# A cached attention and MLP decode step on one core: weight-stage matmuls taken round four column tiles, GELU in thirds, down-projection as four partial sums

## The chip, the cores and the metric

The kernel runs on one core of a Trainium2 chip. The metric is device time in microseconds (us); lower is better. Times quoted are medians of several executions, all of them undisturbed ("fast"). The profile is one further execution, traced; its span is 1 to 2 us shorter than the timed value, because the span runs from the first to the last instruction. Engine names in profile lines: PE is TensorE, PEld its weight loads, DVE is VectorE, ACT is ScalarE, POOL is GpSimd, SP is the engine that issues the large loads.

## The reference, cut to what matters

```python
# x: [8,1,576]   k_cache, v_cache: [8, 32, 4096, 128]   all bf16
g = sigmoid((x * gate_w).sum(-1, keepdims=True))
q = (x @ wq) -> [8, 32 heads, 1, 128]
p = softmax(q @ k_cache^T * 128**-0.5)
a = (p @ v_cache) -> [8,1,4096] @ wo            # attention branch
y = layernorm(x)
h = gelu(y @ w1 + b1)                            # [8,1,4608]
b = h @ w2 + b2                                  # MLP branch
out = g * a + (1 - g) * b
```

The two caches hold 2 x 268 MB = 537 MB. The four weight matrices hold 20 MB. Every byte is used once, so nearly all of the work is reading.

## The kernel before

SBUF holds three slots. The first three loads put wq, w1 and w2 into them; later each slot takes one block of K or V (8.39 MB: eight heads of one batch entry). There are 32 such groups, so 64 block loads, all issued by SP in order, each as soon as the slot that it overwrites is free:

```python
def load_kv(kind, g):
    n = n_load[0]; n_load[0] += 1
    s = n % 3                                        # three slots in turn
    ...
    land[kind, g] = op("sync", lambda e: e.dma_start(slot[s][:, :, :], src), free[n - 3], dma=dma)
```

The order is K0, K1, V0, K2, V1, K3, V2 and so on. K0 takes wq's slot (free when Q is done), K1 takes w1's (free when the up-projection is done), V0 takes w2's (free when the down-projection is done).

The part that the change rewrites is the weight stage, which comes before the first scores. All its matmuls have only 8 useful output rows (the batch), so four results are kept side by side on PSUM partitions 0, 32, 64 and 96. Those are the four *column tiles* of the array:

```python
    for half in range(2):                            # Q projection
        for h in range(4):                           # column tile
            for kt in range(NKT):                    # 5 matmuls in a row on one tile
                o = tr_ps[half][32 * h:32 * h + B, :]
                ... matmul(o, lhsT=xT_sb[:, xi, :], rhs=wq part, start=(kt == 0), stop=(kt == NKT - 1))
    ...
    for k in range(3):                               # up-projection
        for c in range(4):                           # column tile
            o = up_ps[32 * c:32 * c + B, k, 0:FB]
            for kt in range(NKT):                    # 5 matmuls, 128 rows high
                ... matmul(o, lhsT=yT_sb[:, yi, :], rhs=w1 part, start=(kt == 0), stop=False)
            p_up = matmul(o, lhsT=one1[:, :], rhs=b1_row[:, col:col + FB], start=False, stop=True)  # bias: 1 row high
    ...
    # GELU of all of h at once: 4 VectorE passes of 104x1152, a sigmoid on ScalarE, 1 VectorE pass
    # 36 small matmuls transpose h; 4 VectorE copies
    for jt in range(NJ):                             # down-projection, already round the four tiles
        p_down = quarters(hT_sb[:, jt, :], w2_sb[:, jt, :], jt == 0, False, ...)
```

In the loop, one group multiplies K by q on VectorE (8 pieces), sums over the head dimension with matmuls against the identity, reduces on VectorE, finds the maximum, takes exp on ScalarE and multiplies by V on TensorE. The softmax had six small VectorE operations in a chain, one of which only changed a sign.

Of the kernel before, what the change touches and what calls it, by code (L numbers as in the profile page):

```python
# [5 lines left out]
ACT = mybir.ActivationFunctionType  # L6
# [5 lines left out]
B = 8  # L12
# [178 lines left out]
def bass_gated_mix__mha_block_cached__mixer_channel_mlp__decode_kernel(  # L191
# [76 lines left out]
    b2_8 = late.take([B, D])  # L268
    b2_f = late.take32([B, D])
# [6 lines left out]
    zs = sb("zs", [32, 1], F32)  # L276
    acc = sb("acc", [128, GL, HB], F32)
# [11 lines left out]
    diag2 = sb("diag2", [B, 2, B], F32)  # L289
    g4 = sb("g4", [128, 2], F32)  # L290
    g32 = sb("g32", [32, 2, B], F32)
    ident = sb("ident", [128, 128], BF16)
    hneg = sb("hneg", [128, HB], F32)
# [5 lines left out]
    mC = sb("mC", [128, 32], F32)  # L299
# [5 lines left out]
    rz = sb("rz", [128, 1], F32)  # L305
# [11 lines left out]
    g32_ps = bank[3][0:32, 64:64 + 2 * B]  # L317
    ht_ps = PS[:, 0:NJ * 32].rearrange("p (j c b) -> p j c b", j=NJ, c=4)
    xt_ps = bank[7]
# [30 lines left out]
    ld_b2 = load("scalar", b2_8, bcast(B_b2, 0, D), "ld_b2")  # L350
# [55 lines left out]
    c_hneg = op("vector", lambda e: e.tensor_scalar(out=hneg[:, :], in0=hsel[:, ::NDQ], scalar1=-1.0, scalar2=60000.0,  # L406
# [10 lines left out]
    c_selq = op("vector", lambda e: e.tensor_copy(  # L417
# [4 lines left out]
    c_b2 = op("gpsimd", lambda e: e.tensor_copy(out=b2_f, in_=b2_8), [ld_b2])  # L422
    c_sp8 = op("vector", lambda e: e.tensor_copy(
# [4 lines left out]
    c_Sel = op("vector", lambda e: e.tensor_copy(  # L428
# [36 lines left out]
    def untransposed(dst, col, waits):  # L465
        return op("vector", lambda e: e.tensor_copy(
            out=dst.rearrange("p k b -> p (k b)"), in_=xt_ps[:, col:col + (NKF + 2) * B]), waits)
# [9 lines left out]
    v_dg = op("vector", lambda e: e.tensor_tensor(  # L477
        out=diag2[:], in0=bass.AP(tensor=ident, offset=0, ap=[[pstride(ident), B], [0, 2], [1, B]]),
        in1=bass.AP(tensor=stat, offset=G_COL, ap=[[pstride(stat), B], [1, 2], [0, B]]), op=ALU.mult), [v_omg, c_id])
# [5 lines left out]
    t = op("tensor", lambda e: e.matmul(g32_ps, lhsT=ones8[:, :], rhs=diag2[:].rearrange("k s b -> k (s b)"),  # L485
                                        start=True, stop=True), [c_one8])
    v_g4 = op("vector", lambda e: e.tensor_copy(out=g4[:, :], in_=g4_ps), [t])
    v_g32 = op("vector", lambda e: e.tensor_copy(out=g32[:].rearrange("p s b -> p (s b)"), in_=g32_ps), [t])
# [3 lines left out]
    for half in range(2):  # L492
        for h in range(4):
            for kt in range(NKT):
# [12 lines left out]

    for k in range(3):
        for c in range(4):
            col = c * FC + k * FB  # L510
            o = up_ps[32 * c:32 * c + B, k, 0:FB]
            for kt in range(NKT):
                r = w1_sb[:, kt, col:col + FB] if kt < NKF else w1_t[:, col - (c // 2) * (F // 2):][:, 0:FB]
                yi = kt if kt < NKF else NKF + c // 2
                p_up = op("tensor", lambda e, o=o, r=r, kt=kt, yi=yi: e.matmul(  # L515
                    o, lhsT=yT_sb[:, yi, :], rhs=r, start=(kt == 0), stop=False),
                    [v_yT, *ld_w1, *c_ps] if c == kt == k == 0 else ())
            p_up = op("tensor", lambda e, o=o, col=col: e.matmul(  # L518
                o, lhsT=one1[:, :], rhs=b1_row[:, col:col + FB], start=False, stop=True), [ld_b1, c_one1])
    free[1] = [p_up]  # L520
    h = up_ps[0:QP, :, 0:FB]
    t3 = t2[0:QP, :].rearrange("p (k n) -> p k n", k=3)
    t = op("vector", lambda e: e.tensor_copy(out=t3, in_=h), [p_up])  # L523
    t = op("vector", lambda e: e.tensor_tensor(out=t3, in0=t3, in1=h, op=ALU.mult), [t])
    t = op("vector", lambda e: e.tensor_scalar(out=t3, in0=t3, scalar1=0.044715, scalar2=1.0, op0=ALU.mult, op1=ALU.add), [t])
    t = op("vector", lambda e: e.tensor_tensor(out=t3, in0=t3, in1=h, op=ALU.mult), [t])
    t = op("scalar", lambda e: e.activation(out=t3, in_=t3, func=ACT.Sigmoid, scale=gelu_c), [t])
    v_h = op("vector", lambda e: e.scalar_tensor_tensor(
        out=hrow[0:QP, :].rearrange("p (k n) -> p k n", k=3), in0=h, scalar=g4[0:QP, 1:2], in1=t3,
        op0=ALU.mult, op1=ALU.mult), [t, v_g4])  # L530
    v_hb, v_hrow = [v_h], [v_h]
# [9 lines left out]
    def quarters(lhsT, w, first, stop, waits):  # L541

        for i in range(4):
            last = op("tensor", lambda e, i=i: e.matmul(  # L544
                y_ps[32 * i:32 * i + B, 0:QN], lhsT=lhsT, rhs=w[:, i * QN:(i + 1) * QN], start=first, stop=stop),
                waits if i == 0 else ())
        return last

    for jt in range(NJ):
        p_down = quarters(hT_sb[:, jt, :], w2_sb[:, jt, :], jt == 0, False,  # L550
                          [ld_w2, *v_hT, v_yT] if jt == 0 else ())
    for i in range(4):
        p_b2 = op("tensor", lambda e, i=i: e.matmul(
            y_ps[32 * i:32 * i + B, 0:QN], lhsT=diag2[:, 1, :], rhs=b2_f[:, i * QN:(i + 1) * QN], start=False, stop=False),
            [c_b2, v_dg])
    free[2] = [p_b2]
# [242 lines left out]
```

## Time and profile before

| | before |
|---|---|
| time, median of 6 runs | 1295.47 us |
| profiled span | 1293.2 us |
| read from memory | 556.96 MB |
| TensorE, VectorE busy | 57%, 63% |
| DMA share and rate, 5 to 1285 us | 1.00, 433 GB/s |
| first scores start | 59.9 us |

The page of the kernel before. Its first line gives busy time, share of the span and instruction counts; the second is the DMA's busy share in 40 slices, in tenths; the last shows which engines make up the chain of waits that ended last.

```profile
PE 733.4 (57%) x4926; PEld 337.1 (26%) x4926; DVE 819.7 (63%) x873; ACT 161.0 (12%) x587; POOL 40.4 (3%) x60
DMA  9999999999999999999999999999999999999998
HBM read 556.96 MB, written 0.01 MB: 431 GB/s over the span
DMA 54%; DVE 26%; PE 14%; ACT 5%; issue 1%; SPq 0%; ACTq 0%; DVEq 0%
```

No compute engine is busy for more than two thirds of the time, and the DMA row has no hole before its last slice. The last line invites a mistake. It gives VectorE 26% and TensorE 14% of the chain, as if 40% of the span could be had by speeding them up.

The table by windows of the kernel before: stretch, its length, busy time (and instructions) of PE, PEld, DVE, ACT and POOL, TensorE's granted clock, DMA share, GB/s.

```profile
5.00:1285.00 1280.00, 729.89 (x4791) 334.43 (x4792) 816.87 (x867) 159.16 (x584) 38.48 (x46) 0.85 1.00 433
1288.00:1290.00 2.00, 1.57 (x92) 1.19 (x80) 0.00 (x0) 0.00 (x0) 0.00 (x0) 1.00 0.49 191
1290.00:1294.00 4.00, 0.31 (x12) 0.11 (x8) 0.59 (x2) 0.54 (x2) 0.00 (x0) 0.98 0.02 4
```

From 5 to 1285 us the 16 DMA engines have no free time at all. After about 1290 us they have nothing left to do. So the span is roughly 2 us before the bytes flow, 1287 us of full DMA, and 3 us of last arithmetic and the store of the result.

The timeline of the kernel before, weight stage: start, duration, engine, source line, operation, output and inputs, shapes, count, and in brackets the engine's idle time before it and what ended that.

```profile
14.99 5.59 PE L499 MATMUL PS<-SL 128*8 128x512 bf16 x40 [1.01 <-DMA SL<-in_A_wq_dram]
...
32.45 0.98 PE L515 MATMUL PS<-SL 128*8 128x384 bf16 x5
33.36 0.32 PE L518 MATMUL PS<-SL,one 1*8 1x384 bf16 x1
33.61 0.98 PE L515 MATMUL PS<-SL 128*8 128x384 bf16 x5
...
54.97 3.96 PE L544 MATMUL PS<-SL 128*8 128x144 bf16 x144 [2.07 <-DVE SL L538]
...
59.50 0.28 ACT L572 ACTIVATE q_bc<-PS 128x128 bf16<-128x128 f32 x1 [10.41 <-PE PS L569]
...
59.89 4.49 DVE L580 TENSOR_TENSOR SL<-SL,q_bc 128x4096 bf16<-128x4096 bf16 x2 [5.06 <-DMA SL<-in_A_k_cache_dram]
```

L499 is the Q projection, L515 the up-projection, L518 its bias, L544 the down-projection, L572 the copy that makes the first q ready, and L580 the first multiplication of K by q.

The timeline of SP in the kernel before: the issues of K and V blocks. The first line merges two issues; the second of them starts at 20.62 + 22.68 - 0.33 = 42.97 us.

```profile
20.62 22.68 SPq L384 DMA_DIRECT2D SL<-in_A_k_cache_dram  x2
59.34 0.33 SPq L384 DMA_DIRECT2D SL<-in_A_v_cache_dram  x1
84.42 0.33 SPq L384 DMA_DIRECT2D SL<-in_A_k_cache_dram  x1
111.47 0.33 SPq L384 DMA_DIRECT2D SL<-in_A_v_cache_dram  x1
```

One block takes 8.39 MB / 433 GB/s = 19.4 us to move. In the loop a K block takes 43.4 us (median) from issue to landing, so a load spends over half of that waiting behind the loads before it. That is the mistake hidden in the chain of waits: the chain steps from a load back to whatever freed its slot, although the load would not have landed any sooner if the slot had come free earlier.

### The profile page before, as it was taken

To read this page: it belongs to the slowest core of one execution; us is meant where nothing else is said; L and a number is where in the kernel's file an instruction comes from. 1 tells how busy PE (TensorE), PEld (TensorE's weight loads), DVE (VectorE), ACT (ScalarE), POOL (GpSimd) and SP (SyncE) were. 2 spreads that over 40 slices of the span, in tenths; PEclk is the share of its full clock that TensorE was granted. 3 is DMA by queue.
4 is the path that set the end of the run, shared out by engine and by line. 5 is a ranking of instruction groups with operands and counts; after the bars stand their busy time and mean duration, and the time that the engine had idled before them with its cause. 6 is when DMAs were issued, how large, how long until landed. Compare 5 with 4: busy or idle time off the path is not lost.

```text
span 1293.2 us, 11790 instructions
## 1 busy us (share of the span) xinstructions
PE 733.4 (57%) x4926; PEld 337.1 (26%) x4926; DVE 819.7 (63%) x873; ACT 161.0 (12%) x587; POOL 40.4 (3%) x60
## 2 busy tenths in 40 slices
PE   3666566555556555556555556555556555556646
PEld 1322223122223222223222223222223222223223
DVE  2387567665567665567665567765567765567762
ACT  1011110111110011110011110011111011111011
POOL 1001000000000000000000000000000000000000
PEclk8799898878898887898787899778888877888888
DMA  9999999999999999999999999999999999999998
GB/s 406 427 447 424 439 430 436 432 430 436 434 428 436 436 432 438 430 438 432 430 436 434 428 436 438 430 438 430 438 430 432 436 432 434 432 438 430 436 424 366
DMA packets 10591, 557.16 MB, mean 431 GB/s; under 512 B 1201, under 2 KB 1233, under 8 KB 1745
## 3 DMA queue, kind: packets, MB, share of 16 engines
q1 hardware_dynamic: 10528, 556.94, 99.6%
q8 instruction: 9, 0.15, 0.0%
q10 hardware_dynamic: 50, 0.04, 0.0%
q14 instruction: 4, 0.03, 0.0%
HBM read 556.96 MB, written 0.01 MB: 431 GB/s over the span
## 4 chain that ended last, share of the span: by engine, by line
DMA 54%; DVE 26%; PE 14%; ACT 5%; issue 1%; SPq 0%; ACTq 0%; DVEq 0%
DMA SL<-in_A_k_cache_dram 50%; DVE SL L580 20%; PE PS L585 7%; DVE s_sb L591 5%; ACT P L625 4%; PE PS L640 4%; DMA SL<-in_B_w_dram 2%; DMA SL<-in_A_wo_dram 2%; PE PS L515 1%; PE PS L656 1%; ACT O_sb L645 1%; PE PS L544 0%; PE PS L518 0%; PE PS L649 0%; PE PS L535 0%
## 5 line engine op out<-in xcount | busy, mean ns | idle before, releaser
L585 PE MATMUL PS<-SL,ident 128*128 128x512 bf16 x2048 | 547.7, 420 | 518.3 <-DVE SL L580 518.3
L580 DVE TENSOR_TENSOR SL<-SL,q_bc 128x4096 bf16<-128x4096 bf16 x256 | 582.0, 2284 | 313.6 <-DMA SL<-in_A_k_cache_dram 313.6
L585 PEld LDWEIGHTS PS<-SL,ident 128*128 128x128 bf16 x2048 | 199.0, 106 | 853.8 <-DVE SL L580 614.8
L591 DVE TENSOR_REDUCE s_sb<-PS 128x32 f32<-128x512 f32 x256 | 175.8, 687 | 90.4 <-PE PS L585 90.3
L625 ACT ACTIVATE P<-s_sb,hb 128x256 bf16<-128x256 f32 x256 | 126.2, 494 | 663.3 <-PE PS L640 645.5
L640 PE MATMUL PS<-SL,P 128*32 128x512 bf16 x2048 | 128.5, 389 | 0.0
L640 PEld LDWEIGHTS PS<-SL,P 128*32 128x32 bf16 x2048 | 96.4, 138 | 17.9 <-issue 3.1
L564 POOL TENSOR_SCALAR Qm<-Q,sel 128x256 bf16<-128x256 bf16 x33 | 33.7, 1020 | 896.6 <-ACT O_sb L645 845.2
L572 ACT ACTIVATE q_bc<-PS 128x128 bf16<-128x128 f32 x33 | 9.1, 277 | 407.4 <-PE PS L569 407.4
L625 ACT ACTIVATION_READ_ACCUMULATOR P<-s_sb,hb 128x1 f32 x256 | 47.7, 186 | 0.0
L656 PE MATMUL PS<-O_sb,selq 128*32 128x128 f32 x256 | 34.2, 278 | 0.7 <-ACT O_sb L645 0.7
L656 PEld LDWEIGHTS PS<-O_sb,selq 128*32 128x32 f32 x256 | 26.0, 113 | 1.4 <-ACT O_sb L645 1.2
L645 ACT ACTIVATE O_sb<-PS 128x512 f32<-128x512 f32 x32 | 18.4, 574 | 10.0 <-PE PS L640 10.0
L523 DVE COPY SL<-PS 104x1152 f32<-104x1152 f32 x1 | 1.4, 1357 | 28.7 <-PE PS L518 28.7
L515 PE MATMUL PS<-SL 128*8 128x384 bf16 x60 | 13.2, 356 | 6.8 <-DMA SL<-in_B_w_dram 6.8
L669 DVE SCALAR_TENSOR_TENSOR On<-PS,rz,dqm 32x128 f32<-32x128 f32 x32 | 10.9, 339 | 9.0 <-PE PS L656 7.9
L683 POOL TENSOR_TENSOR OT<-OTs,g 32x96 bf16<-32x96 f32 (+2 forms) x12 | 4.2, 347 | 320.3 <-DVE OTs L673 320.2
L610 DVE TENSOR_REDUCE mA<-s_sb 128x1 f32<-128x256 f32 x32 | 13.4, 420 | 1.1
L673 DVE TENSOR_REDUCE OTs<-On 32x32 f32<-32x128 f32 x32 | 12.1, 378 | 1.1
L649 PE MATMUL PS<-acc,hsel 128*32 128x8 f32 x64 | 7.4, 188 | 5.9 <-ACT O_sb L645 4.7
L663 DVE TENSOR_REDUCE zs<-PS 32x1 f32<-32x8 f32 x32 | 4.7, 147 | 8.2 <-PE PS L656 7.9
L649 PEld LDWEIGHTS PS<-acc,hsel 128*32 128x32 f32 x64 | 4.5, 110 | 19.5 <-issue 12.7
(82 smaller groups left out, 114.5 us busy)
## 6 DMA issues: line engine op xcount, KB each, us to landing
SL<-in_A_v_cache_dram SPq DMA_DIRECT2D x2, 4096.0 KB, 38.4
SL<-in_B_w_dram SPq DMA_DIRECT2D x1, 5184.0 KB, 37.7
SL<-in_B_w_dram SPq DMA_DIRECT2D x1, 4608.0 KB, 24.1
SL<-in_A_wq_dram SPq DMA_DIRECT2D x1, 4096.0 KB, 13.0
SL<-in_A_wo_dram SPq DMA_DIRECT2D x1, 3456.0 KB, 22.0
SL<-in_A_wo_dram SPq DMA_DIRECT2D x1, 864.0 KB, 23.7
SL<-in_B_w_dram SPq DMA_DIRECT2D x1, 576.0 KB, 25.0
SL<-in_A_wq_dram SPq DMA_DIRECT2D x1, 512.0 KB, 13.6
```

Of the source, the lines that this page charges most:

```text
L515: p_up = op("tensor", lambda e, o=o, r=r, kt=kt, yi=yi: e.matmul(o, lhsT=yT_sb[:, yi, :], rhs=r, start=(kt == 0), stop=False), [v_yT, *ld_ ...
L564: g_qm[g] = op("gpsimd", lambda e: e.tensor_scalar(out=Qm[:, :, :].rearrange("p k d -> p (k d)"), in0=Q4[:, 2 * hg * DH:(2 * hg + 2) * DH] ...
L580: v_mult[g, c] = op("vector", lambda e: e.tensor_tensor(out=part, in0=part, in1=qb, op=ALU.mult), [land["k", g], a_qb[g]], token="tensor" ...
L585: p_sum[g, c] = op("tensor", lambda e, r=r, n=n: e.matmul(tr_ps[par][:, :], lhsT=ident[:, :], rhs=r, start=(n == 0), stop=(n == NCH - 1)), ...
L591: v_red[g, c] = op("vector", lambda e: e.tensor_reduce(out=s_sb[:, c * CT:(c + 1) * CT], in_=tr_ps[par][:, :].rearrange("p (t c) -> p t c" ...
L610: t = op("vector", lambda e: e.tensor_reduce(out=mA[:, 0:1], in_=s_sb[:, :], axis=AX.X, op=ALU.max), [v_red[g, NCK - 1], c_mA], token=own)
L625: a_exp[g] = op("scalar", lambda e, h=h: e.activation(out=P[:, :, h, :], in_=s_sb[:, :].rearrange("p (s t) -> p s t", s=2), func=ACT.Exp, ...
L640: p_pv[g] = op("tensor", lambda e, o=o, lhsT=lhsT, rhs=rhs, tq=tq: e.matmul(o, lhsT=lhsT, rhs=rhs, start=(tq < 4), stop=(tq >= NTQ - 4)), ...
L645: a_ev[g] = op("scalar", lambda e: e.activation(out=O_sb[:].rearrange("p t d -> p (t d)"), in_=o_ps[:, :], func=ACT.Copy), [p_pv[g], p_z.g ...
L649: p_z[g] = op("tensor", lambda e: e.matmul(oz_ps[0:32, DH:DH + HB], lhsT=hsel[:, :], rhs=acc[:, place(g), :], start=True, stop=True), [a_e ...
L656: p_oz[g] = op("tensor", lambda e, tt=tt: e.matmul(oz_ps[0:32, 0:DH], lhsT=selq[:, tt, :], rhs=O_sb[:, tt, :], start=(tt == 0), stop=(tt = ...
L673: v_norm[g] = op("vector", lambda e: e.tensor_reduce(out=OTs[:, :, place(g + 2)], in_=On[:, :].rearrange("p (q j) -> p j q", q=NDQ), axis= ...
```

## The change

The intent was a shorter weight stage: Q and up-projection matmuls alternate over the four column tiles, so that four of them can run at once; the bias matmuls of a third come together after its 20 others; GELU starts on a third of h while TensorE computes the next; the down-projection makes four partial sums with w2 as the moving operand, 288 columns wide. Small copies move from VectorE to ScalarE, the sign change leaves the softmax, and the copies of the result wait for their own quarter only.

```diff
     for half in range(2):
-        for h in range(4):
-            for kt in range(NKT):
+        for kt in range(NKT):
+            for h in range(4):
 ...
     for k in range(3):
-        for c in range(4):
-            col = c * FC + k * FB
-            o = up_ps[32 * c:32 * c + B, k, 0:FB]
-            for kt in range(NKT):
+        at = [(c, c * FC + k * FB, up_ps[32 * c:32 * c + B, k, 0:FB]) for c in range(4)]
+        for kt in range(NKT):
+            for c, col, o in at:
                 r = w1_sb[:, kt, col:col + FB] if kt < NKF else ...
                 ... matmul(o, lhsT=yT_sb[:, yi, :], rhs=r, start=(kt == 0), stop=False)
+        for c, col, o in at:
             p_up = ... matmul(o, lhsT=one1[:, :], rhs=b1_row[:, col:col + FB], start=False, stop=True)
+        ... GELU of this third ...
 ...
-    for jt in range(NJ):
-        p_down = quarters(hT_sb[:, jt, :], w2_sb[:, jt, :], jt == 0, False, ...)
+    for j0 in range(0, NJ, 4):
+        for k in range(2):
+            for c in range(4):
+                jt = j0 + c
+                p_down = ... matmul(b_ps[32 * c:32 * c + B, k, 0:D // 2], lhsT=hT_sb[:, jt, :],
+                                    rhs=w2_sb[:, jt, k * (D // 2):(k + 1) * (D // 2)], ...)
+    v_b = ... VectorE: b_sb = b2 * (1 - g) + b_ps
+    for i in range(4):
+        p_y = ... matmul that adds up the four partial sums
 ...   softmax:
-        t = op("vector", lambda e: e.tensor_scalar(out=mC..., in0=gmb, scalar1=-1.0, ...), [t], token=own)
-        t = op("vector", lambda e: e.transpose(mD[:, :], mC[:, :]), [t], token=own)
+        t = op("vector", lambda e: e.transpose(mD[:, :], gmb), [t], token=own)
```

More of the change, by code (lines that the diff above doesn't have):

```diff
@@ L267, in bass_gated_mix__mha_block_cached__mixer_channel_mlp__decode_kernel @@
     hT_sb = late.take([128, NJ, B])
-    b2_8 = late.take([B, D])
-    b2_f = late.take32([B, D])
+    b2_z = late.take([128, D])
+    b_sb = late.take32([128, D])
     t2 = late.take32([128, FC])
@@ L276, in bass_gated_mix__mha_block_cached__mixer_channel_mlp__decode_kernel @@
     zs = sb("zs", [32, 1], F32)
+    rz = sb("rz", [32, 1], F32)
     acc = sb("acc", [128, GL, HB], F32)
@@ L288, in bass_gated_mix__mha_block_cached__mixer_channel_mlp__decode_kernel @@
     one1 = sb("one1", [1, B], BF16)
-    diag2 = sb("diag2", [B, 2, B], F32)
+    diag = sb("diag", [B, B], F32)
     g4 = sb("g4", [128, 2], F32)
-    g32 = sb("g32", [32, 2, B], F32)
+    g32 = sb("g32", [32, B], F32)
     ident = sb("ident", [128, 128], BF16)
-    hneg = sb("hneg", [128, HB], F32)
+    hpos = sb("hpos", [128, HB], F32)
     sel32 = sb("sel32", [128, HB, TQ], F32)
@@ L298, in bass_gated_mix__mha_block_cached__mixer_channel_mlp__decode_kernel @@
     mB = sb("mB", [128, 32], F32)
-    mC = sb("mC", [128, 32], F32)
     mD = sb("mD", [128, 32], F32)
@@ L304, in bass_gated_mix__mha_block_cached__mixer_channel_mlp__decode_kernel @@
     O_sb = sb("O_sb", [128, TQ, DH], F32)
-    rz = sb("rz", [128, 1], F32)
     PS = nc.alloc_psum_tensor("PS", [128, 8 * 512], F32)
@@ L316, in bass_gated_mix__mha_block_cached__mixer_channel_mlp__decode_kernel @@
     g4_ps = bank[3][:, 0:2]
-    g32_ps = bank[3][0:32, 64:64 + 2 * B]
+    g32_ps = bank[3][0:32, 64:64 + B]
     ht_ps = PS[:, 0:NJ * 32].rearrange("p (j c b) -> p j c b", j=NJ, c=4)
+    b_ps = PS[:, 5 * 512:7 * 512].rearrange("p (k n) -> p k n", k=2)
     xt_ps = bank[7]
@@ L349, in bass_gated_mix__mha_block_cached__mixer_channel_mlp__decode_kernel @@
     ld_b1 = load("scalar", b1_row, bass.AP(tensor=B_b1.tensor, offset=B_b1.offset, ap=[[F, 1], [1, F]]), "ld_b1")
-    ld_b2 = load("scalar", b2_8, bcast(B_b2, 0, D), "ld_b2")
+    c_b2 = op("gpsimd", lambda e: e.memset(b2_z, 0.0))
+    ld_b2 = load("scalar", b2_z[0:B, :], bcast(B_b2, 0, D), "ld_b2", [c_b2])
     def kv_src(cache, g):
@@ L405, in bass_gated_mix__mha_block_cached__mixer_channel_mlp__decode_kernel @@
                                                     base=PH - 1, pattern=[[PH, HB], [0, NDQ]], channel_multiplier=-1), [t])
-    c_hneg = op("vector", lambda e: e.tensor_scalar(out=hneg[:, :], in0=hsel[:, ::NDQ], scalar1=-1.0, scalar2=60000.0,
+    c_hpos = op("vector", lambda e: e.tensor_scalar(out=hpos[:, :], in0=hsel[:, ::NDQ], scalar1=-1.0, scalar2=-60000.0,
                                                     op0=ALU.add, op1=ALU.mult), [c_hsel])
@@ L416, in bass_gated_mix__mha_block_cached__mixer_channel_mlp__decode_kernel @@
         axis=AX.X, op=ALU.add), [c_id])
-    c_selq = op("vector", lambda e: e.tensor_copy(
+    c_selq = op("scalar", lambda e: e.copy(
         out=selq[:].rearrange("p t (h q) -> p t h q", q=NDQ),
@@ L421, in bass_gated_mix__mha_block_cached__mixer_channel_mlp__decode_kernel @@
     c_one1 = memset("gpsimd", one1[:], 1.0)
-    c_b2 = op("gpsimd", lambda e: e.tensor_copy(out=b2_f, in_=b2_8), [ld_b2])
-    c_sp8 = op("vector", lambda e: e.tensor_copy(
+    c_sp8 = op("scalar", lambda e: e.copy(
         out=spread8[:].rearrange("b (c r) -> b c r", c=4),
@@ L427, in bass_gated_mix__mha_block_cached__mixer_channel_mlp__decode_kernel @@
         out=Rows[:], in_=ident[:, :].rearrange("p (h r) -> p h r", h=4), axis=AX.X, op=ALU.add), [c_id])
-    c_Sel = op("vector", lambda e: e.tensor_copy(
+    c_Sel = op("scalar", lambda e: e.copy(
         out=Sel[:].rearrange("p (h r) -> p h r", h=4),
@@ L465, in untransposed @@
     def untransposed(dst, col, waits):
-        return op("vector", lambda e: e.tensor_copy(
+        return op("scalar", lambda e: e.copy(
             out=dst.rearrange("p k b -> p (k b)"), in_=xt_ps[:, col:col + (NKF + 2) * B]), waits)
@@ L476, in bass_gated_mix__mha_block_cached__mixer_channel_mlp__decode_kernel @@
                                                    scalar1=-1.0, scalar2=1.0, op0=ALU.mult, op1=ALU.add), [a_g])
-    v_dg = op("vector", lambda e: e.tensor_tensor(
-        out=diag2[:], in0=bass.AP(tensor=ident, offset=0, ap=[[pstride(ident), B], [0, 2], [1, B]]),
-        in1=bass.AP(tensor=stat, offset=G_COL, ap=[[pstride(stat), B], [1, 2], [0, B]]), op=ALU.mult), [v_omg, c_id])
+    v_dg = op("vector", lambda e: e.tensor_scalar(
+        out=diag[:, :], in0=ident[0:B, 0:B], scalar1=stat[:, G_COL:G_COL + 1], scalar2=None, op0=ALU.mult), [v_omg, c_id])
     v_yz = spread(yz, y_sb, [v_y])
@@ L484, in bass_gated_mix__mha_block_cached__mixer_channel_mlp__decode_kernel @@
            [v_dg, c_sp8])
-    t = op("tensor", lambda e: e.matmul(g32_ps, lhsT=ones8[:, :], rhs=diag2[:].rearrange("k s b -> k (s b)"),
+    t = op("tensor", lambda e: e.matmul(g32_ps, lhsT=ones8[:, :], rhs=diag[:, :],
                                         start=True, stop=True), [c_one8])
-    v_g4 = op("vector", lambda e: e.tensor_copy(out=g4[:, :], in_=g4_ps), [t])
-    v_g32 = op("vector", lambda e: e.tensor_copy(out=g32[:].rearrange("p s b -> p (s b)"), in_=g32_ps), [t])
+    v_g4 = op("scalar", lambda e: e.copy(out=g4[:, :], in_=g4_ps), [t])
+    v_g32 = op("scalar", lambda e: e.copy(out=g32[:, :], in_=g32_ps), [t])
     a_Q = []
@@ L505, in bass_gated_mix__mha_block_cached__mixer_channel_mlp__decode_kernel @@
     load_kv("k", 0)
+    v_hrow = []
     for k in range(3):
-        for c in range(4):
-            col = c * FC + k * FB
-            o = up_ps[32 * c:32 * c + B, k, 0:FB]
-            for kt in range(NKT):
+        at = [(c, c * FC + k * FB, up_ps[32 * c:32 * c + B, k, 0:FB]) for c in range(4)]
+        for kt in range(NKT):
+            for c, col, o in at:
                 r = w1_sb[:, kt, col:col + FB] if kt < NKF else w1_t[:, col - (c // 2) * (F // 2):][:, 0:FB]
                 yi = kt if kt < NKF else NKF + c // 2
-                p_up = op("tensor", lambda e, o=o, r=r, kt=kt, yi=yi: e.matmul(
+                op("tensor", lambda e, o=o, r=r, kt=kt, yi=yi: e.matmul(
@@ L516, in bass_gated_mix__mha_block_cached__mixer_channel_mlp__decode_kernel @@
                     o, lhsT=yT_sb[:, yi, :], rhs=r, start=(kt == 0), stop=False),
                     [v_yT, *ld_w1, *c_ps] if c == kt == k == 0 else ())
+        for c, col, o in at:
             p_up = op("tensor", lambda e, o=o, col=col: e.matmul(
                 o, lhsT=one1[:, :], rhs=b1_row[:, col:col + FB], start=False, stop=True), [ld_b1, c_one1])
-    free[1] = [p_up]
-    h = up_ps[0:QP, :, 0:FB]
-    t3 = t2[0:QP, :].rearrange("p (k n) -> p k n", k=3)
-    t = op("vector", lambda e: e.tensor_copy(out=t3, in_=h), [p_up])
@@ L524, in bass_gated_mix__mha_block_cached__mixer_channel_mlp__decode_kernel @@
-    t = op("vector", lambda e: e.tensor_tensor(out=t3, in0=t3, in1=h, op=ALU.mult), [t])
-    t = op("vector", lambda e: e.tensor_scalar(out=t3, in0=t3, scalar1=0.044715, scalar2=1.0, op0=ALU.mult, op1=ALU.add), [t])
-    t = op("vector", lambda e: e.tensor_tensor(out=t3, in0=t3, in1=h, op=ALU.mult), [t])
-    t = op("scalar", lambda e: e.activation(out=t3, in_=t3, func=ACT.Sigmoid, scale=gelu_c), [t])
-    v_h = op("vector", lambda e: e.scalar_tensor_tensor(
-        out=hrow[0:QP, :].rearrange("p (k n) -> p k n", k=3), in0=h, scalar=g4[0:QP, 1:2], in1=t3,
-        op0=ALU.mult, op1=ALU.mult), [t, v_g4])
@@ L531, in bass_gated_mix__mha_block_cached__mixer_channel_mlp__decode_kernel @@
-    v_hb, v_hrow = [v_h], [v_h]
+        h = up_ps[0:QP, k, 0:FB]
+        t3 = t2[0:QP, k * FB:(k + 1) * FB]
+        t = op("vector", lambda e, t3=t3, h=h: e.tensor_copy(out=t3, in_=h), [p_up])
+        t = op("vector", lambda e, t3=t3, h=h: e.tensor_tensor(out=t3, in0=t3, in1=h, op=ALU.mult), [t])
+        t = op("vector", lambda e, t3=t3: e.tensor_scalar(out=t3, in0=t3, scalar1=0.044715, scalar2=1.0, op0=ALU.mult,
+                                                          op1=ALU.add), [t])
@@ new lines, in bass_gated_mix__mha_block_cached__mixer_channel_mlp__decode_kernel @@
+        t = op("vector", lambda e, t3=t3, h=h: e.tensor_tensor(out=t3, in0=t3, in1=h, op=ALU.mult), [t])
+        t = op("scalar", lambda e, t3=t3: e.activation(out=t3, in_=t3, func=ACT.Sigmoid, scale=gelu_c), [t])
+        v_hrow.append((t, h, t3))
+    free[1] = [p_up]
+    for k, (t, h, t3) in enumerate(v_hrow):
+        v_h = op("vector", lambda e, k=k, h=h, t3=t3: e.scalar_tensor_tensor(
+            out=hrow[0:QP, k * FB:(k + 1) * FB], in0=h, scalar=g4[0:QP, 1:2], in1=t3,
+            op0=ALU.mult, op1=ALU.mult), [t, v_g4])
@@ L533, in bass_gated_mix__mha_block_cached__mixer_channel_mlp__decode_kernel @@
+    v_hrow = [v_h]
     per_quarter = bass.AP(tensor=ident, offset=0, ap=[[pstride(ident), QP], [32, 4], [1, B]])
@@ L539, in bass_gated_mix__mha_block_cached__mixer_channel_mlp__decode_kernel @@
         out=hT_sb[32 * c:32 * c + 32, :, :], in_=ht_ps[0:32, :, c, :]), [p_hT]) for c in range(4)]
-    def quarters(lhsT, w, first, stop, waits):
-        for i in range(4):
-            last = op("tensor", lambda e, i=i: e.matmul(
-                y_ps[32 * i:32 * i + B, 0:QN], lhsT=lhsT, rhs=w[:, i * QN:(i + 1) * QN], start=first, stop=stop),
-                waits if i == 0 else ())
-        return last
-    for jt in range(NJ):
-        p_down = quarters(hT_sb[:, jt, :], w2_sb[:, jt, :], jt == 0, False,
-                          [ld_w2, *v_hT, v_yT] if jt == 0 else ())
+    for j0 in range(0, NJ, 4):
+        for k in range(2):
+            for c in range(4):
+                jt = j0 + c
+                p_down = op("tensor", lambda e, jt=jt, k=k, c=c: e.matmul(
+                    b_ps[32 * c:32 * c + B, k, 0:D // 2], lhsT=hT_sb[:, jt, :], rhs=w2_sb[:, jt, k * (D // 2):(k + 1) * (D // 2)],
+                    start=(jt < 4), stop=(jt >= NJ - 4)), [ld_w2, *v_hT, v_h] if jt == k == 0 else ())
+    v_b = op("vector", lambda e: e.scalar_tensor_tensor(
+        out=b_sb[0:QP, :].rearrange("p (k n) -> p k n", k=2), in0=b2_z[0:QP, :].rearrange("p (k n) -> p k n", k=2),
+        scalar=g4[0:QP, 1:2], in1=b_ps[0:QP, :, 0:D // 2], op0=ALU.mult, op1=ALU.add), [p_down, ld_b2, v_g4])
     for i in range(4):
-        p_b2 = op("tensor", lambda e, i=i: e.matmul(
-            y_ps[32 * i:32 * i + B, 0:QN], lhsT=diag2[:, 1, :], rhs=b2_f[:, i * QN:(i + 1) * QN], start=False, stop=False),
-            [c_b2, v_dg])
-    free[2] = [p_b2]
+        p_y = op("tensor", lambda e, i=i: e.matmul(
+            y_ps[32 * i:32 * i + B, 0:QN], lhsT=sel32[0:QP, :, :].rearrange("p h t -> p (h t)")[:, 0:B],
+            rhs=b_sb[0:QP, i * QN:(i + 1) * QN], start=True, stop=False), [v_b, v_yT, c_sel32])
+    free[2] = [p_y]
     a_qb, v_mult, v_red, p_sum, v_nm, a_exp, p_pv, a_ev, p_z, p_oz, v_norm, g_ot, g_qm, p_q, v_rz = ({} for _ in range(15))
@@ L570, in q_of @@
                 qb_ps[64 * k:64 * k + 64, 0:DH], lhsT=Sel[:, :], rhs=Qm[:, k, :], start=True, stop=True),
-                [g_qm[g], c_Sel, *v_hb, a_qb.get(g - 1)] if k == 0 else (), token="scalar" if looped and k == 1 else None)
+                [g_qm[g], c_Sel, v_h, a_qb.get(g - 1)] if k == 0 else (), token="scalar" if looped and k == 1 else None)
         a_qb[g] = op("scalar", lambda e: e.activation(out=q_bc[:, place(g), :], in_=qb_ps[:, 0:DH], func=ACT.Copy),
@@ L615, in softmax @@
         gmb = bass.AP(tensor=gm, offset=0, ap=[[pstride(gm), 128], [1, 2], [0, PH]])
-        t = op("vector", lambda e: e.tensor_scalar(out=mC[:, :].rearrange("p (k r) -> p k r", k=2), in0=gmb,
-                                                   scalar1=-1.0, scalar2=None, op0=ALU.mult), [t], token=own)
-        t = op("vector", lambda e: e.transpose(mD[:, :], mC[:, :]), [t], token=own)
-        v_nm[g] = op("vector", lambda e: e.tensor_scalar(out=hb8[:, :], in0=hneg[:, :], scalar1=mD[:, 0:1], scalar2=None,
-                                                         op0=ALU.add), [t, c_hneg, a_exp.get(g - 1)],
+        t = op("vector", lambda e: e.transpose(mD[:, :], gmb), [t], token=own)
+        v_nm[g] = op("vector", lambda e: e.tensor_scalar(out=hb8[:, :], in0=hpos[:, :], scalar1=mD[:, 0:1], scalar2=-1.0,
+                                                         op0=ALU.add, op1=ALU.mult), [t, c_hpos, a_exp.get(g - 1)],
                      token="scalar" if in_loop(g) else None)
@@ L650, in row_sums @@
             oz_ps[0:32, DH:DH + HB], lhsT=hsel[:, :], rhs=acc[:, place(g), :], start=True, stop=True),
-            [a_ev[g] if g < NG - 1 else a_ev[g - 1], v_norm.get(g - 1), c_hsel, *v_hb])
+            [a_ev[g] if g < NG - 1 else a_ev[g - 1], v_norm.get(g - 1), c_hsel, v_h])
     def gather(g):
@@ L758, in bass_gated_mix__mha_block_cached__mixer_channel_mlp__decode_kernel @@
     place_o("vector", last - 1, last + 1)
+    p_a = {}
     for j in range(NJO):
-        p_a = quarters(OT[:, j, :], wo_sb[:, j, :], False, j == NJO - 1, [ld_wo[j], *g_ot.values()])
-    parts = [op("vector" if i < 2 else "scalar", lambda e, i=i: (e.tensor_copy if i < 2 else e.copy)(
-        out_sb[:, i * QN:(i + 1) * QN], y_ps[32 * i:32 * i + B, 0:QN]), [p_a]) for i in range(4)]
+        for i in range(4):
+            p_a[i] = op("tensor", lambda e, i=i, j=j: e.matmul(
+                y_ps[32 * i:32 * i + B, 0:QN], lhsT=OT[:, j, :], rhs=wo_sb[:, j, i * QN:(i + 1) * QN], start=False,
+                stop=(j == NJO - 1)), [ld_wo[j], *g_ot.values()])
+    parts = [op("vector" if i % 2 == 0 else "scalar", lambda e, i=i: (e.tensor_copy if i % 2 == 0 else e.copy)(
+        out_sb[:, i * QN:(i + 1) * QN], y_ps[32 * i:32 * i + B, 0:QN]), [p_a[i]]) for i in range(4)]
     ld_out = [load("sync", out_flat, out_sb[:, :], "ld_out", parts)]
```

## The prediction

> **What bounds the kernel now.** The DMA engines. The table by windows gives a DMA share of 1.00 at 433 GB/s from 5 to 1285 us; TensorE is busy 57%, VectorE 63% (page, part 1). The span reads 556.96 MB (part 3): at 433 GB/s an estimated 1286 of the 1293.2 us. The rest is about 2 us before bytes flow and 3 us after the last (share 0.00 in 1290 to 1292). The chain of waits puts 26% on VectorE and 14% on TensorE, but it follows a load back to what freed its slot, although an issued load then queues: 43.4 us to landing (part 6), while 8.39 MB at 433 GB/s take 19.4 us. The Trainium skill, "DMA: Bandwidth & Descriptors", section "Bandwidth", puts the ceiling of 16 engines at 435 GB/s; this trace's 433 agrees.
>
> **What the change does** (timeline, first 60 us):
> - Q projection: 40 matmuls take 5.6 us, 140 ns each, five in a row on one column tile. Where the kernel already goes round the four tiles (probabilities times V, 64 matmuls of the same 512 columns in 3.5 us) one takes 55 ns. The skill's "TensorEngine Tiling (Array Packing)", section "Theoretical Speedup", allows up to 4x at 32 columns. Estimate: 2.2 to 3 us.
> - Up-projection: 27.3 to 42.9 us, 72 matmuls of 384 columns; estimate 3 to 6 us (clock 0.50 at its start).
> - GELU: 7.6 us after the last matmul; in thirds about 4 us stay exposed.
> - Down-projection already went round the tiles (148 matmuls, 4.4 us); 72 of 288 columns stream as many columns, so no gain; a VectorE sum (0.7 us) and four small matmuls are added.
> - Small copies move to ScalarE; one VectorE operation (0.18 us) leaves each softmax.
>
> The weight stage should end near 46 us instead of 59.3. The second K block is then issued near 33 us instead of 43.0, the first V block near 46 instead of 59.3.
>
> **How much is critical.** Almost nothing. Those loads only join a longer queue: by bytes, weights (15.3 MB) and first K block (8.4 MB) keep the engines busy to about 57 us, the second K block to about 77 us. The first scores may start 2 to 3 us earlier, near 57, but later ones are paced by landings, which don't move; 38.7 us per turn of the loop is exactly two loads. In the tail, the output waits for the last pieces of wo; the new order of copies saves perhaps 0.1 us. No bytes are removed.
>
> **Predicted time:** 1295.3 us, range 1292.8 to 1297.5. Faster by over 2%: 0.01; within 2%: 0.985; slower: 0.005.
>
> **What would show each step right.** DMA share 1.00 at 433 GB/s unchanged; up-projection over by 33 us; the first V load issued 10 to 15 us earlier, with a time to landing longer by as much; from the third head group and batch on, multiplications by K starting within 1 us of before; last bytes near 1290 us; TensorE idling longer ahead of the scores.
>
> **What would make it wrong.** A gap in the DMA hidden by the trace's bursts (one round of packets is about 2.4 us, so a 2 us slice can show 131 GB/s without a gap), which an earlier issue would fill: up to 2 us faster. Deeper queueing or concurrent TensorE reads lowering the DMA rate: some us slower.

## More of the kernel before

In the up-projection, each group of five and its bias take 1.16 us (33.61 - 32.45), even at the full clock. The first scores wait for two things that come within a tenth of a microsecond of each other: q is ready at 59.78 us, and the first K block, issued at 20.62 us with 39.2 us to landing, is there at 59.8 us. The profile names only the later one, the DMA.

## The result, and the profile after

| | before | after |
|---|---|---|
| time, median of 6 runs each | 1295.47 us | 1294.89 us |
| ratio of after to before | | 0.9994, 95% interval 0.9981 to 1.0006 |
| profiled span | 1293.2 us | 1293.1 us |
| up-projection over | 42.9 us | 32.2 us |
| first V load issued | 59.3 us | 47.8 us |
| first scores start | 59.9 us | 59.6 us |
| DMA share and rate, 5 to 1285 us | 1.00, 433 GB/s | 1.00, 433 GB/s |

A ratio is the mean time of one kernel's fast runs over the mean of the other's fast runs in the same rounds, so it is not quite the ratio of the medians. The two kernels are the same within the interval.

The page after, lines as before:

```profile
PE 721.8 (56%) x4854; PEld 330.1 (26%) x4854; DVE 814.6 (63%) x845; ACT 164.0 (13%) x597; POOL 39.7 (3%) x60
DMA  9999999999999999999999999999999999999998
HBM read 556.96 MB, written 0.01 MB: 431 GB/s over the span
DMA 56%; DVE 25%; PE 13%; ACT 5%; issue 1%; SPq 0%; ACTq 0%; DVEq 0%
```

TensorE is busy 11.6 us less and VectorE 5.1 us less, while bytes, DMA row and rate are the same. The chain's DMA part has grown from 54% to 56% in a span of the same length.

The windows after:

```profile
5.00:1285.00 1280.00, 718.71 (x4723) 327.95 (x4724) 812.26 (x839) 162.22 (x594) 37.21 (x45) 0.84 1.00 433
1288.00:1290.00 2.00, 1.58 (x92) 1.21 (x80) 0.00 (x0) 0.00 (x0) 0.00 (x0) 1.00 0.41 156
1290.00:1294.00 4.00, 0.32 (x12) 0.10 (x8) 0.60 (x2) 0.54 (x2) 0.00 (x0) 0.90 0.01 2
```

The timeline after, weight stage (L498 is Q, L514 and L518 the up-projection and its bias, L548 the down-projection, L574 the copy that makes the first q ready, L582 the first multiplication by q):

```profile
14.80 4.44 PE L498 MATMUL PS<-SL 128*8 128x512 bf16 x40 [1.12 <-DMA SL<-in_A_wq_dram]
27.16 1.77 PE L514 MATMUL PS<-SL 128*8 128x384 bf16 x20 [7.92 <-DMA SL<-in_B_w_dram]
...
30.93 0.99 PE L514 MATMUL PS<-SL 128*8 128x384 bf16 x20
31.85 0.33 PE L518 MATMUL PS<-SL,one 1*8 1x384 bf16 x4
...
41.62 4.49 PE L548 MATMUL PS<-SL 128*8 128x288 bf16 x72 [2.07 <-DVE SL L541]
...
47.99 0.28 ACT L574 ACTIVATE q_bc<-PS 128x128 bf16<-128x128 f32 x1 [11.82 <-PE PS L571]
...
59.58 4.49 DVE L582 TENSOR_TENSOR SL<-SL,q_bc 128x4096 bf16<-128x4096 bf16 x2 [12.61 <-DMA SL<-in_A_k_cache_dram]
```

The stage is shorter by 11.6 us: q is ready at 48.27 us instead of 59.78. The last line shows where that went. The first K block lands at 59.6 us, as good as unmoved, and VectorE idles until then (12.61 us) and starts its multiplications 0.3 us earlier than before. The 5.06 us of idle time in the kernel before were spent waiting for q as much as for the K block.

The issues of SP after. The second K issue is at 19.28 + 13.27 - 0.33 = 32.22 us:

```profile
19.28 13.27 SPq L385 DMA_DIRECT2D SL<-in_A_k_cache_dram  x2
47.76 0.33 SPq L385 DMA_DIRECT2D SL<-in_A_v_cache_dram  x1
84.58 0.33 SPq L385 DMA_DIRECT2D SL<-in_A_k_cache_dram  x1
111.13 0.33 SPq L385 DMA_DIRECT2D SL<-in_A_v_cache_dram  x1
```

The first V load is issued 11.6 us earlier, and takes 50.5 us to landing instead of 39.2 us, 11.3 us longer. From K2 on, no issue has moved by more than 0.44 us. Deep in the loop, one multiplication by q starts at 1201.64 us before and at 1201.65 us after.

### The profile page after: what moved, and what is told of

Its sections match the earlier page's. It is cut to its first block, busy times and chain, and to the rows that moved or that the text cites. A ratio compares the mean times of both kernels' runs of the same rounds, so it can differ in the third digit from the quotient of the medians.

```text
span 1293.1 us, 11630 instructions
## 1 busy us (share of the span) xinstructions
PE 721.8 (56%) x4854; PEld 330.1 (26%) x4854; DVE 814.6 (63%) x845; ACT 164.0 (13%) x597; POOL 39.7 (3%) x60
## 4 chain that ended last, share of the span: by engine, by line
DMA 56%; DVE 25%; PE 13%; ACT 5%; issue 1%; SPq 0%; ACTq 0%; DVEq 0%
DMA SL<-in_A_k_cache_dram 53%; DVE SL L582 20%; PE PS L587 7%; DVE s_sb L593 5%; ACT P L625 4%; PE PS L640 4%; DMA SL<-in_A_wo_dram 2%; DMA SL<-in_A_wq_dram 1%; PE PS L656 1%; ACT O_sb L645 1%; PE PS L498 0%; PE PS L649 0%; SPq L326 0%; DVE mA L612 0%; PE PS L762 0%
## 5 line engine op out<-in xcount | busy, mean ns | idle before, releaser
L582 DVE TENSOR_TENSOR SL<-SL,q_bc 128x4096 bf16<-128x4096 bf16 x256 | 581.8, 2283 | 328.8 <-DMA SL<-in_A_k_cache_dram 328.8
L574 ACT ACTIVATE q_bc<-PS 128x128 bf16<-128x128 f32 x33 | 9.2, 277 | 420.2 <-PE PS L571 420.2
L514 PE MATMUL PS<-SL 128*8 128x384 bf16 x60 | 4.2, 430 | 7.9 <-DMA SL<-in_B_w_dram 7.9
```

The costliest lines, as they stand in the source:

```text
L582: v_mult[g, c] = op("vector", lambda e: e.tensor_tensor(out=part, in0=part, in1=qb, op=ALU.mult), [land["k", g], a_qb[g]], token="tensor" ...
```

## The experiments

The theory: the DMA engines are full in both kernels, so that a shorter weight stage only lengthens the queue; what it gains is reserve. A first rival: the gain is real on the clock and is given back later on the engines, by new waits or a slower DMA. A second question came up on the way: what in the weight stage gained the time.

### 1. The loads alone

All computation is taken out; the loads stay in their order, each waiting for the landing of the load three before it. The output is zeros.

```diff
-    ... weight stage, loop, output projection ...
+    for kind, g in order:                        # K0, K1, V0, K2, V1, ...
+        landed[n] = [load("sync", slot[s][:, :, :], src, ..., landed[n - 3])]
+    last = [load("sync", wo_sb[...], ..., landed[n - 3]) for the three parts of wo]
+    out = zeros
```

> Only the loads of the changed kernel, in their order and with its three slots; each load waits for the landing of the load three before it and nothing is computed (the output is zeros, wrong on purpose). Theory (the DMA engines are full from start to end in both kernels): 1292 to 1295 us, at most 3 us under the changed kernel. Rival (waits of the loads for compute cost time, and the change gave its gain back there): under 1285 us.

Measured: 1292.62 us, 2.3 us (0.18%) under the changed kernel, whose time is from other rounds. The kernel before took 1296.22 us beside this run; the ratio to it is 0.9974 (95% interval 0.9958 to 0.9991). The windows of this run:

```profile
5.00:1285.00 1280.00, 0.00 (x0) 0.00 (x0) 1.00 1.00 433
1288.00:1290.00 2.00, 0.00 (x0) 0.00 (x0) 1.00 0.05 13
```

(With only VectorE and POOL present, the columns after the length are their two busy times, clock, share and rate.) With no computation at all the DMA has the same share and the same rate. All arithmetic of the kernel together costs 2 to 3 us, of which about 1 us is the last matmuls and copies after the last bytes (the store of the result is issued 2.3 us later than in this run). A rearrangement of the computation has no more than that to win while these bytes are read in this order through three slots. The rival needed this run under 1285 us; it falls.

### 2. Half the DMA, the same computation

Only the first half of each block is loaded, and each half is used twice, so that each engine has as much work as before and the DMA has half. The result is wrong. (The comparison with the reference still reports it as correct, probably because values averaged over thousands of rows of V are too small for its tolerance to notice; so it says nothing here.)

```diff
-        ... e.dma_start(slot[s][:, :, :], src)
+        ... e.dma_start(slot[s][:, 0:NTT // 2, :], src[:, 0:NTT // 2, :])
 ...
-        part = kb[:, c * CT:(c + 1) * CT, :]
+        at = c % (NCK // 2)
+        part = kb[:, at * CT:(at + 1) * CT, :]
 ...
-            rhs = vb[:, s * NTT // 2 + i:(s + 1) * NTT // 2:NTQ // 2, :]
+            rhs = vb[:, i:NTT // 2:NTQ // 2, :]
```

> The kernel before with half of every K and V block loaded and each half used twice (wrong on purpose), so the engines have the same work and the DMA half. Theory: the loop is then paced by VectorE, about 28 to 29 us per turn instead of 38.7, about 980 to 1020 us in all; the first scores still start near 59.8 us, when q is ready.

> The changed kernel with the same halving. Theory (the gain is real, but hidden under the DMA): first scores near 48.5 us, 11.5 us earlier than half_before, and another 0.2 us per turn from the removed softmax operation, 6 to 7 us over 32 turns: 16 to 20 us less than half_before. Rival (the gain is given back on the engines): within 5 us of half_before.

> half_after with the softmax operation put back. Theory: 6 to 7 us more than half_after, so 10 to 12 us less than half_before. If the softmax operation is not on the path of a VectorE-bound loop: the same as half_after.

| kernel | time, median of 4 | first scores start |
|---|---|---|
| half_before | 979.27 us | 61.3 us |
| half_after | 969.55 us | 50.0 us |
| half_after_oldsm | 968.96 us | 50.1 us |

With the DMA out of the way the change is worth 9.7 us. The start of the first scores moves by 11.4 us; by the last scores 10.6 us of it are left, and about 1 us goes in the tail of the profiled runs, where the last multiplication by V ran 6.44 us in half_after and 5.49 us in half_before. So the gain of the weight stage is real, and the rival fails again.

The second half of the expectation missed. The operation removed from the softmax is worth nothing here: putting it back did not slow the kernel. The expectation took VectorE to pace the turn. The timeline of half_before at the end of one turn shows another chain:

```profile
532.62 3.67 PE L637 MATMUL PS<-SL,P 128*32 128x512 bf16 x61
533.92 0.23 DVE L616 TENSOR_SCALAR hb<-hneg,mD 128x8 f32<-128x8 f32 x1
536.41 0.51 ACT L622 ACTIVATE P<-s_sb,hb 128x256 bf16<-128x256 f32 x1 [21.60 <-PE PS L637]
540.56 0.69 DVE L588 TENSOR_REDUCE s_sb<-PS 128x32 f32<-128x512 f32 x1 [0.60 <-ACT P L622]
```

The softmax's last VectorE operation (hb) is ready at 534.15 us, but exp on ScalarE starts at 536.41, when TensorE has finished multiplying the previous probabilities by V, since both use the one buffer P. The reduction on VectorE then waits for exp to have read s_sb. The turn of 27.8 us is closed through TensorE, ScalarE and VectorE, and the softmax operations have some 2 us of slack in it.

### 3. Delays put into the weight stage

20 or 40 clears of an unused PSUM bank are put on VectorE between GELU and the transposition of h, in the kernel before and in the changed one. This measures how much later the stage may end before the time notices.

```diff
+    for _ in range(20):          # or 40
+        v_hrow = [op("vector", lambda e: e.memset(PS[:, 3 * 512:4 * 512], 0.0), [*v_hrow, v_g4, v_g32])]
```

> The kernel before with 20 dummy VectorE clears of one PSUM bank between GELU and the transposition of h, an estimated 10 us. Theory: q is ready near 70 us, the first scores start 10 us later, and as the first two turns are paced by VectorE the V block issued at 111.5 us comes 10 us later into a queue that has about 4 to 5 us of work left at that moment: 5 to 7 us slower than the kernel before. If the weight stage were critical one for one: 10 us slower; if wholly hidden: the same.

> The same 20 clears in the changed kernel. Theory: q is ready near 58 us instead of 48, still before the first K block lands at 59.6 us: the same time as the changed kernel within 1 us. Rival (the earlier end of the stage does count): 5 us slower or more.

> 40 clears, an estimated 20 us, in the kernel before. Theory: first scores near 80 us, 14 to 17 us slower than the kernel before.

> 40 clears in the changed kernel. Theory: q ready near 68 us, 8.7 us after the first K block lands, of which 4 to 5 us are absorbed by the queue: 3 to 6 us slower than the changed kernel, 10 to 13 us faster than delay40_before.

The kernel before took 1294.94 us beside these runs; the changed kernel's time is that of the result above.

| kernel | first scores start | time, median of 4 | slower than without delay |
|---|---|---|---|
| before | 59.9 us | 1294.94 us | |
| delay20_before | 74.8 us | 1305.92 us | 11.0 us |
| delay40_before | 90.9 us | 1321.43 us | 26.5 us |
| changed | 59.6 us | 1294.89 us | |
| delay20_after | 61.5 us | 1295.19 us | 0.3 us |
| delay40_after | 75.5 us | 1306.93 us | 12.0 us |

The losses of three runs are larger than expected, because the delays were: one clear is busy 0.48 us, but with the wait between two of them one took 0.67 us, so 20 took 13.3 us and not the estimated 10. With the measured start times the picture is the expected one: what is lost is the lateness of the first scores minus roughly a constant. 74.8 - 59.9 - 11.0 = 3.9 us; 90.9 - 59.9 - 26.5 = 4.5 us; 75.5 - 59.6 - 12.0 = 3.9 us. The constant is known only roughly, because the start times come from the profiled executions and the losses from medians: the four runs of delay40_before fell into two pairs, near 1319.3 and near 1323.6 us, and with the spans of the profiled executions (1305.7, 1322.1 and 1306.3 us) it is 2.1 to 2.7 us. It fits the work that the DMA queue still has when the second V block is issued: up to that moment, 111.47 us, the trace of the kernel before shows 427 GB/s, 47.6 MB of the 48.9 MB issued, which leaves an estimated 3 us. In delay20_before the holes can be seen in the windows:

```profile
95.00:100.00 5.00, 3.50 (x16) 1.21 (x14) 3.61 (x4) 0.00 (x0) 0.00 (x0) 1.00 0.12 52
120.00:125.00 5.00, 3.20 (x15) 1.19 (x14) 4.59 (x4) 0.00 (x0) 0.00 (x0) 1.00 0.00 0
```

In the kernel before, both windows have a share of 0.97. Over 95 to 100 us (share 0.12) and 118 to 126 us (0.25) the idle time of the DMA adds up to 10.4 us, nearly all of the 11.0 us lost. So 20 clears cost the old kernel 11.0 us and the changed one 0.3 us. The change has bought a reserve of some 11 us (from q at 48.27 us to the landing at 59.6 us), and nothing in this kernel uses it.

### 4. What shortened the weight stage

The timelines suggested the order of the column tiles. Two kernels change only that order, both with half the DMA so that a difference would show.

```diff
 # half_before_neworder: half_before with           # half_after_oldorder: half_after with
-        for c in range(4): ... for kt in range(NKT):
+        for kt in range(NKT): for c in range(4):           (and the reverse in half_after_oldorder)
```

> half_before (half the DMA, result wrong on purpose) with only the order of the Q and up-projection matmuls changed, nothing else. If the order is what shortens the weight stage, as the timelines suggest (up-projection 5.0 instead of 15.6 us): up-projection over near 32.5 us, q ready near 50 us instead of 61, 8 to 11 us less than half_before. If the split GELU and the new down-projection carry half of it: 4 to 6 us less.

> half_after with only the order of the Q and up-projection matmuls put back. If the order is what counts: up-projection over near 43 us, q ready near 58 us, 7 to 10 us more than half_after; the split GELU keeps some 2 to 3 us. If the rest carries half of it: 4 to 6 us more.

Measured: half_before_neworder 968.85 us, as expected; half_after_oldorder 968.92 us, nothing lost, a clear miss. Its up-projection, with five in a row on one tile, ran from 27.3 to 34.8 us. The two results fit together only if the order alone is not what matters, and the code shows what else differed: the bias matmuls. In the old kernel each stood between two groups of five. In half_before_neworder they had moved behind all 20 along with the new order, and in half_after_oldorder I had left them there. A bias matmul is 1 row high, the others are 128 rows high.

The Trainium skill, page "TensorEngine Tiling (Array Packing)", section "Tiling Modes", Key Properties, says that changing the tiling mode, not just the tile, drains TensorE. That a 1-row matmul among 128-row ones is such a change is a guess here. Two more kernels test whether the height is what counts. The first leaves order and places of half_before alone and only makes the bias matmuls 128 rows high, with zeros under the bias row. (Clearing the larger bias tile takes GpSimd 3.94 us at the start, and the Q projection starts at 17.80 instead of 14.83 us; the up-projection still waits for w1 and starts at 27.12 us.) The second keeps the new order, but puts each 1-row bias straight behind the last matmul of its tile.

```diff
 # half_before_bias128
-    b1_row = late.take([1, F])
+    b1_row = late.take([128, F])                   # cleared, then the bias loaded into row 0
-    one1 = sb("one1", [1, B], BF16)
+    one1 = sb("one1", [128, B], BF16)              # ones in row 0, zeros below
```

```diff
 # half_after_biasback
         for kt in range(NKT):
             for c, col, o in at:
                 ... matmul, 128 rows ...
-        for c, col, o in at:
-            p_up = ... bias matmul, 1 row ...
+                if kt == NKT - 1:
+                    p_up = ... bias matmul, 1 row ...
```

> half_before with the 12 bias matmuls of the up-projection at their old places, one after every five, but 128 rows high (zeros below the bias row) instead of 1 row. half_after_oldorder had shown 7.5 us for the up-projection with five in a row but the bias matmuls gathered, against 15.6 us with them in between. Theory (going from 128 rows to 1 row and back makes the array wait): up-projection 7 to 9 us, about 7 us less in all than half_before. Rival (anything between, or the row of five on one column tile): 15 to 16 us, time as half_before.

> half_after, round the four tiles as in the change, but each one-row bias matmul straight after the last matmul of its tile, so 24 changes of height instead of 6. Theory: 18 changes more at (15.6 - 7.5) / 18 = 0.45 us each, up-projection near 13 us instead of 5, 4 to 8 us more in all than half_after, as the split GELU hides part. Rival (the order of the tiles is what counts): 5 to 6 us, time as half_after.

| kernel | order of tiles | changes of height | up-projection | one third at clock 0.50 | time |
|---|---|---|---|---|---|
| half_before | five in a row | 24 | 16.6 us | 8.4 us | 979.27 us |
| half_before_bias128 | five in a row | none | 6.9 us | 2.4 us | 969.03 us |
| half_after_oldorder | five in a row | 6 | 7.5 us | 3.0 us | 968.92 us |
| half_before_neworder | round the tiles | 6 | 6.1 us | 2.1 us | 968.85 us |
| half_after | round the tiles | 6 | 6.4 us | 2.1 us | 969.55 us |
| half_after_biasback | round the tiles | 24 | 13.8 us | 4.6 us | 972.48 us |

(The up-projection is counted from its first matmul to the end of its last bias matmul.) These totals mix two clocks: the granted clock was 0.50 when the up-projection began in all six, and rose to 1.00 within it at different moments, in half_after and half_after_biasback not at all. So the fifth column compares one third, 20 matmuls and four bias matmuls, in a stretch whose granted clock was 0.50; for half_before and half_before_bias128 it is four times one group of five with its bias (2.10 and 0.60 us).

With no or few changes of height the order matters little: 2.4 and 3.0 us against 2.1 us. With 24 of them it matters much: 8.4 us against 4.6 us. So both count together. Where 1-row matmuls stand between the groups of five, a group runs alone: five matmuls of one tile took 1.76 us in half_before, as long as 20 matmuls round the four tiles in half_after (1.77 us), both at clock 0.50. The first group in the timeline of half_before:

```profile
27.18 1.76 PE L511 MATMUL PS<-SL 128*8 128x384 bf16 x5 [7.18 <-DMA SL<-in_B_w_dram]
```

The timeline of half_before_bias128, at the full clock, has five matmuls of one tile and the bias in 0.33 us, start to start, where the kernel before took 1.16 us:

```profile
32.36 0.50 PE L513 MATMUL PS<-SL 128*8 128x384 bf16 x5
32.68 0.33 PE L516 MATMUL PS<-SL,one 128*8 128x384 bf16 x1
32.69 0.50 PE L513 MATMUL PS<-SL 128*8 128x384 bf16 x5
33.01 0.33 PE L516 MATMUL PS<-SL,one 128*8 128x384 bf16 x1
```

The timeline of half_after_biasback shows the opposite, single matmuls and bias matmuls alternating at 0.41 us each, at clock 0.50:

```profile
29.23 0.48 PE L510 MATMUL PS<-SL 128*8 128x384 bf16 x1
29.64 0.48 PE L514 MATMUL PS<-SL,one 1*8 1x384 bf16 x1
30.05 0.48 PE L510 MATMUL PS<-SL 128*8 128x384 bf16 x1
```

Without the changes of height, the array works on several groups of five at once by itself: six matmuls in 0.33 us is 55 ns each, the same as the 52 ns of the changed kernel's last third (24 in 1.25 us). The order of the tiles then adds next to nothing. What these runs show is that 1-row matmuls between 128-row ones keep groups from overlapping; that the array drains at each change is the page's account of it, which no trace here shows directly. The time of half_after_biasback, 2.9 us over half_after, is under the 4 to 8 us that were expected; its four runs fell into two pairs, near 970.7 and near 974.5 us, and the profiled run was like the slower pair. Four of the six kernels end at about 969 us, and their times cannot rank them: the scores start between 50.0 and 51.2 us in all four. In half_after and half_after_oldorder the first K half-block comes last, about 50 us, however early q is ready; in half_before_neworder and half_before_bias128 it is q.

## Why the prediction was right, and where it was not

- **What bounds the kernel.** Right. Share 1.00 at 433 GB/s is unchanged, and the loads alone take 1292.62 us. The Trainium skill's ceiling of 435 GB/s for the 16 ports that the engines share ("DMA: Bandwidth & Descriptors", section "Bandwidth") agrees with all three traces.
- **The time.** Predicted 1295.3 us, measured 1294.89 us, inside the range. The difference of 0.4 us is inside the scatter of the runs.
- **The weight stage.** Up-projection over by 32.2 us (predicted 33), first V load issued at 47.8 us (predicted 46). The up-projection took 5.0 us (predicted 3 to 6). Of the 11.6 us, 10.8 come from the earlier end of the up-projection. GELU's exposed part fell from 7.7 to 5.1 us (predicted: about 4 left), and the stretch from the first down-projection matmul to the matmul that makes q grew from 4.25 to 6.00 us, the price of the sum on VectorE and the four matmuls behind it. The shorter Q projection gave nothing to the stage, because the up-projection then waits for w1 (27.34 us before, 27.16 us after).
- **The Q projection was mis-sized.** Predicted 2.2 to 3 us, measured 4.44 us. The estimate took its pace (55 ns) from a stretch in the middle of the kernel. Here four matmuls of 512 columns took 0.43 us, 107 ns each, half that pace. The Trainium skill, page "TensorE: Matmul & The Clock Gate", Part 1, describes a clock at half rate until TensorE has been busy for about 3.4 us; the trace agrees in its effect, as the up-projection's first 24 matmuls took 2.11 us and the last 24 took 1.25 us. The granted clock in the windows of this profile does not show it: it reads 1.00 in both stretches. In half_after the same first 24 matmuls took 2.12 us and the granted clock reads 0.50, so it seems to be the record of this profile that is off. For the Q projection every profile reads 1.00.
- **The named cause was not enough.** The prediction put the slow old pace down to "five in a row on one column tile". In the up-projection that order alone is not slow: section 4 shows 2.4 to 3.0 us a third with it at clock 0.50 when the bias matmuls are made 128 rows high or gathered, against 8.4 us with them 1 row high between the groups. The size came out right by luck, because the change also gathered the bias matmuls; the new order with each bias straight behind its tile took 4.6 us a third and not 2.1. In the Q projection, which has no bias, the order accounts for about 1 us: 5.59 against 4.44 us, and with only the order changed 5.17 against 4.43 us (half_before, half_before_neworder).
- **The first scores: wrong.** Predicted near 57 us, 2 to 3 us earlier than before; measured 59.6 us, 0.3 us earlier. By bytes the first K block should be complete at 57; VectorE could start on it 2.5 us later. One round of packets is an estimated 2.4 us (16 of 65.5 KB at 433 GB/s), but what makes the landing late was not tested.
- **Later groups within 1 us.** Right: 117.7 against 117.9 us for the third group, 1201.65 against 1201.64 us late in the loop.
- **A gap in the DMA hidden by bursts.** There was none: the loads alone and the changed kernel have the same rate.
- **Hidden, not given back.** With half the DMA the weight stage is worth 9.7 us; with all of it some 11 us appear as reserve against delays.

## What to carry to other kernels

Before speeding up a stage, look whether the DMA share over the long middle of the kernel is 1.00; if it is, take the bytes over the measured rate as the floor, and a kernel of the loads alone as its proof. A chain of waits that runs through compute engines does not make them the bound when each load waits in the queue for longer than it takes to move. And when one edit does two things, as a new loop order that also gathers the odd-shaped matmuls, undo them one at a time before naming the cause, and compare stretches at the same granted clock.

## What the Trainium skill lacked or had wrong

- "TensorEngine Tiling (Array Packing)", section "Tiling Modes": says that changing the mode drains TensorE, but gives no size. Here a 1-row and a 128-row matmul of 384 columns alternated at 0.41 us each at clock 0.50, and 24 changes of height made the up-projection, with five in a row on each tile, 9.7 us longer (16.6 against 6.9 us, part of it at half clock). The page does not name the case of a 1-row bias matmul among others.
- The same page, section "Performance Considerations", could say that matmuls on different column tiles overlap even if issued five in a row per tile: groups of six took 0.33 us, 55 ns a matmul, with no round-robin order, as long as no matmul of another height stood between them.
- "TensorE: Matmul & The Clock Gate", Part 1: the granted clock of the profile read 1.00 over 14 to 20 us after the change, while the matmuls ran at half pace (107 ns for a 512-column matmul, four tiles at once, against 55 ns later). In half_after the first 24 matmuls of the up-projection took as long as in this profile (2.12 and 2.11 us) with 0.50 on record instead of 1.00. The page warns that the records can be unreliable; no run here shows why.
- "DMA: Bandwidth & Descriptors", section "Bandwidth", gives 425 GB/s measured at 16 MB, issued from GpSimd; loads of 8.39 MB kept queued ran at 433 GB/s here over 1280 us.
